# Layer scale, x + gamma * y: rows laid out in HBM as contiguous blocks of 4, 64 and 60 rows per partition

## The chip, the cores and the metric

One core of one Trainium2 chip; the other cores are idle. The metric is the device time of one execution in microseconds (us), the median of the runs. A profiled execution also has a span, which is 1.3 us shorter than the time of that same execution, and a record of every instruction and DMA packet. A profile is of one execution, which can be faster or slower than the median. All runs in this text are of the fast state, at a granted clock of 1.0.

## The reference

```python
B, S, D = 1024, 16, 512
x, y:  bf16 (B, S, D), normal * 0.05
gamma: bf16 (D), 1e-4 * normal * 0.05
def reference(x, y, gamma):
    return x + gamma * y
```

That is 16,384 rows of 1 KB each for x, for y and for the output: 50.3 MB of traffic with two vector operations on it.

## The kernel before

Each of the 128 partitions holds 128 rows. The kernel is hand-scheduled: a list of transfers for each of the two queues (SP loads, ACT stores) and a list of VectorE operations. A tuple `('x', 64, 117, 0)` is a load of rows 64 to 116 of every partition to place 0 of the x buffer, so it has to wait for the add that frees that place.

```python
PIECES = [53, 11, 53, 11]                # rows of the vector operations
SP = [('y', 0, 4), ('y', 4, 64), ('x', 0, 64, 0), ('y', 64, 128), ('x', 64, 117, 0), ('x', 117, 128, 64)]
ACT = [('g',), ('s', 0, 64), ('s', 64, 128)]
EARLY = (2, 0)                           # the first two loads go out at the very start
RELEASE = ('x', 64, 117, 0)              # its landing releases the stores
DVE = [('m', 0), ('m', 1), ('a', 0), ('a', 1), ('m', 2), ('m', 3), ('a', 2), ('a', 3)]
# ...
xv = xf.rearrange("(p n) d -> p n d", p=P)     # partition p: rows 128p .. 128p+127
yv = yf.rearrange("(p n) d -> p n d", p=P)     # so partitions are 128 KB apart
ov = of.rearrange("(p n) d -> p n d", p=P)
# ... in ring(), for each transfer, after its wait:
i = eng.dma_start(out=to, in_=xv[:, w[1] : w[2], :]).then_inc(s_load[w], 16)
# ... in the VectorE loop:
nc.vector.tensor_tensor(out=yt, in0=yt, in1=g, op=MULT)     # "m": y * gamma, in place
nc.vector.tensor_tensor(out=yt, in0=xt, in1=yt, op=ADD)     # "a": + x, in place
```

A transfer of R rows becomes 128 packets, one per partition, each of R KB; the 16 DMA engines take 8 packets each.

## Time and profile before

| | before |
|---|---|
| time, median of 3 runs when the prediction was made | 119.94 us (119.78 to 120.6) |
| span of the profiled run | 118.7 us |
| bytes, mean rate over the span | 50.33 MB, 424 GB/s |
| VectorE busy | 70.0 us (59%) |
| DMA packets per engine, without gamma | 8 transfers x 8 = 64 |

The prediction below shows the slices, the windows and the timeline. One more view of the same profile: the DMA issues of the page. The columns are the transfer, the issuing queue, the number of such transfers, the size of one, and the us from issue to landing, where landing is the moment the slowest of the 16 engines is done.

```profile
y_sb<-in_y_dram SPq DMA_DIRECT2D x1, 7680.0 KB, 21.4
x_sb<-in_x_dram SPq DMA_DIRECT2D x1, 6784.0 KB, 20.8
...
y_sb<-in_y_dram SPq DMA_DIRECT2D x1, 512.0 KB, 3.8
```

The last line is the 4-row piece, the first is the 60-row piece queued behind it, and the second is the late x load. A long landing time is mostly waiting in the queue behind other transfers.

### The profile page before, as it was taken

To read this page: it belongs to the slowest core of one execution; us is meant where nothing else is said; L and a number is where in the kernel's file an instruction comes from. 1 tells how busy PE (TensorE), PEld (TensorE's weight loads), DVE (VectorE), ACT (ScalarE), POOL (GpSimd) and SP (SyncE) were. 2 spreads that over 40 slices of the span, in tenths; PEclk is the share of its full clock that TensorE was granted. 3 is DMA by queue.
4 is the path that set the end of the run, shared out by engine and by line. 5 is a ranking of instruction groups with operands and counts; after the bars stand their busy time and mean duration, and the time that the engine had idled before them with its cause. 6 is when DMAs were issued, how large, how long until landed. Compare 5 with 4: busy or idle time off the path is not lost. (4 is left out here: it accounts for less than half of the span.)

```text
span 118.7 us, 80 instructions
## 1 busy us (share of the span) xinstructions
PE 0.6 (0%) x1; PEld 0.1 (0%) x1; DVE 70.0 (59%) x10; POOL 0.2 (0%) x4
## 2 busy tenths in 40 slices
PE   0001000000000000000000000000000000000000
PEld 0000000000000000000000000000000000000000
DVE  0002000599999299999759999999999910000000
POOL 0000000000000000000000000000000000000000
DMA  8977977998899888998896969498899889988891
GB/s 268 571 332 331 663 331 331 596 464 353 353 486 574 353 353 353 640 420 353 353 585 293 585 293 585 205 634 353 353 596 464 353 353 420 640 353 353 353 663 44
DMA packets 1154, 50.33 MB, mean 424 GB/s; under 512 B 129, under 2 KB 130, under 8 KB 258
## 3 DMA queue, kind: packets, MB, share of 16 engines
q1 hardware_dynamic: 864, 33.55, 66.0%
q10 hardware_dynamic: 290, 16.78, 32.6%
HBM read 33.56 MB, written 16.78 MB: 424 GB/s over the span
## 5 line engine op out<-in xcount | busy, mean ns | idle before, releaser
L156 DVE TENSOR_TENSOR y_sb<-y_sb,gamma_sb 128x27136 bf16<-128x27136 bf16 (+1 forms) x4 | 34.6, 8688 | 12.3 <-DVEq L25 12.3
L165 DVE TENSOR_TENSOR y_sb<-x_sb,y_sb 128x27136 bf16<-128x27136 bf16 (+1 forms) x4 | 34.6, 8689 | 2.3 <-DVEq L25 2.2
L132 DVE CAST gamma_sb<-gamma_ps 128x512 bf16<-128x512 f32 x1 | 0.7, 692 | 8.8 <-DVEq L25 8.8
L127 DVE MEMSET ones_row<- 1x128 bf16 x1 | 0.2, 165 | 2.0 <-PEq L41 2.0
L130 PE MATMUL gamma_ps<-gamma_row,ones_row 1*128 1x512 bf16 x1 | 0.6, 577 | 10.2 <-PEq L25 10.2
L130 PEld LDWEIGHTS gamma_ps<-gamma_row,ones_row 1*128 1x128 bf16 x1 | 0.1, 99 | 10.2 <-issue 10.2
L194 POOL MEMSET const-bfloat16-1.0<- 128x1 bf16 x1 | 0.1, 101 | 0.0
L194 POOL MEMSET const-uint8-127<- 128x1 uint8 x1 | 0.1, 101 | 0.0
L194 POOL MEMSET const-float32-0.0<- 128x1 f32 x1 | 0.1, 98 | 0.2 <-issue 0.2
L194 POOL MEMSET const-float32-1.0<- 128x1 f32 x1 | 0.1, 98 | 0.0
## 6 DMA issues: line engine op xcount, KB each, us to landing
y_sb<-in_y_dram SPq DMA_DIRECT2D x1, 7680.0 KB, 21.4
x_sb<-in_x_dram SPq DMA_DIRECT2D x1, 6784.0 KB, 20.8
x_sb<-in_x_dram SPq DMA_DIRECT2D x1, 1408.0 KB, 23.8
y_sb<-in_y_dram SPq DMA_DIRECT2D x1, 512.0 KB, 3.8
out_dram<-y_sb ACTq DMA_DIRECT2D x2, 22.8
x_sb<-in_x_dram SPq DMA_DIRECT2D x1, 39.3
gamma_row<-in_gamma_dram ACTq DMA_DIRECT2D x1, 1.0 KB
y_sb<-in_y_dram SPq DMA_DIRECT2D x1, 58.3
```

The source lines that it names most:

```text
L127: nc.vector.memset(ones_row, 1.0).then_inc(s_ones, 1)
L130: nc.tensor.matmul(gamma_ps, ones_row, gamma_row, start=True, stop=True).then_inc(s_ps, 1)
L132: nc.vector.tensor_copy(out=gamma_sb, in_=gamma_ps).then_inc(s_dve, 1)
L156: nc.vector.tensor_tensor(out=yt, in0=yt, in1=g, op=MULT).then_inc(s_dve, 1)
L165: nc.vector.tensor_tensor(out=yt, in0=xt, in1=yt, op=ADD).then_inc(s_add, 1)
L194: nc = _bacc.Bacc("TRN2", target_bir_lowering=False, num_devices=1)
```

## The change

The intent: every transfer reads or writes one contiguous stretch of HBM, and the small first piece, on which the start depends, is one contiguous 512 KB. x, y and the output have to share the layout, so the 4-row pieces of x and of the output become transfers of their own. The late x rows are cut into 49 and 11.

```diff
+BLOCKS = [4, 64, 60]
+
-PIECES = [53, 11, 53, 11]
+PIECES = [57, 11, 49, 11]
-SP = [('y', 0, 4), ('y', 4, 64), ('x', 0, 64, 0), ('y', 64, 128), ('x', 64, 117, 0), ('x', 117, 128, 64)]
-ACT = [('g',), ('s', 0, 64), ('s', 64, 128)]
+SP = [
+    ('y', 0, 4), ('y', 4, 68), ('x', 0, 4, 0), ('x', 4, 68, 4),      # (one tuple a line in the kernel)
+    ('y', 68, 128), ('x', 68, 117, 0), ('x', 117, 128, 57),
+]
+ACT = [('g',), ('s', 4, 68), ('s', 0, 4), ('s', 68, 128)]
-RELEASE = ('x', 64, 117, 0)
+RELEASE = ('x', 68, 117, 0)
...
-    xv = xf.rearrange("(p n) d -> p n d", p=P)
...
+    def rows_of(t, a, b):
+        c = max(c for c in range(len(BLOCKS)) if edges[c] <= a)
+        block = t[P * edges[c] : P * edges[c + 1]].rearrange("(p n) d -> p n d", p=P)
+        return block[:, a - edges[c] : b - edges[c], :]
...
-                i = eng.dma_start(out=to, in_=xv[:, w[1] : w[2], :]).then_inc(s_load[w], 16)
+                i = eng.dma_start(out=to, in_=rows_of(xf, w[1], w[2])).then_inc(s_load[w], 16)
```

More of the change, by code (lines that the diff above doesn't have):

```diff
@@ L3 @@
 from concourse import mybir
-PIECES = [53, 11, 53, 11]
-SP = [('y', 0, 4), ('y', 4, 64), ('x', 0, 64, 0), ('y', 64, 128), ('x', 64, 117, 0), ('x', 117, 128, 64)]
-ACT = [('g',), ('s', 0, 64), ('s', 64, 128)]
+BLOCKS = [4, 64, 60]
+PIECES = [57, 11, 49, 11]
+SP = [
+    ('y', 0, 4),
+    ('y', 4, 68),
+    ('x', 0, 4, 0),
+    ('x', 4, 68, 4),
+    ('y', 68, 128),
+    ('x', 68, 117, 0),
+    ('x', 117, 128, 57),
+]
+ACT = [('g',), ('s', 4, 68), ('s', 0, 4), ('s', 68, 128)]
 EARLY = (2, 0)
-RELEASE = ('x', 64, 117, 0)
+RELEASE = ('x', 68, 117, 0)
 DVE = [('m', 0), ('m', 1), ('a', 0), ('a', 1), ('m', 2), ('m', 3), ('a', 2), ('a', 3)]
@@ L51 @@
     dt = xf.dtype
-    xv = xf.rearrange("(p n) d -> p n d", p=P)
-    yv = yf.rearrange("(p n) d -> p n d", p=P)
-    ov = of.rearrange("(p n) d -> p n d", p=P)
+    edges = [sum(BLOCKS[:c]) for c in range(len(BLOCKS) + 1)]
+    assert edges[-1] == rows
+    def rows_of(t, a, b):
+        c = max(c for c in range(len(BLOCKS)) if edges[c] <= a)
+        assert b <= edges[c + 1]
+        block = t[P * edges[c] : P * edges[c + 1]].rearrange("(p n) d -> p n d", p=P)
+        return block[:, a - edges[c] : b - edges[c], :]
     gamma_row = nc.alloc_sbuf_tensor("gamma_row", [1, D], dt).ap()
@@ L112, in ring @@
                 to = x_sb[:, w[3] : w[3] + w[2] - w[1], :]
-                i = eng.dma_start(out=to, in_=xv[:, w[1] : w[2], :]).then_inc(s_load[w], 16)
+                i = eng.dma_start(out=to, in_=rows_of(xf, w[1], w[2])).then_inc(s_load[w], 16)
             elif kind == "y":
                 r = slice(w[1], w[2])
-                i = eng.dma_start(out=y_sb[:, r, :], in_=yv[:, r, :]).then_inc(s_load[w], 16)
+                i = eng.dma_start(out=y_sb[:, r, :], in_=rows_of(yf, w[1], w[2])).then_inc(s_load[w], 16)
             else:
                 r = slice(w[1], w[2])
-                i = eng.dma_start(out=ov[:, r, :], in_=y_sb[:, r, :]).then_inc(s_out, 16)
+                i = eng.dma_start(out=rows_of(of, w[1], w[2]), in_=y_sb[:, r, :]).then_inc(s_out, 16)
             if k < n_early:
```

## The prediction

> **What bounds the kernel now.** I began with the page of the profile, its second part (40 equal slices of the span) and its DMA part. Each digit of the DMA row is the busy share of the 16 DMA engines in a slice.
>
> ```profile
> DVE  0002000599999299999759999999999910000000
> DMA  8977977998899888998896969498899889988891
> DMA packets 1154, 50.33 MB, mean 424 GB/s; under 512 B 129, under 2 KB 130, under 8 KB 258
> HBM read 33.56 MB, written 16.78 MB: 424 GB/s over the span
> ```
>
> VectorE is idle for the first 22 us and the last 23 us. The DMA row never falls to 0 between the first slice and the last. The digits 4 to 7 in its middle are no holes: a packet of this kernel is up to 64 KB and lasts about 2.4 us, close to the 2.97 us of a slice, and the page books it where it starts or ends. So I asked for wider windows, where this blurs away (the last two columns are the DMA busy share and GB/s):
>
> ```profile
> 4.00:60.00 56.00, 0.58 (x1) 0.10 (x1) 35.28 (x5) 0.00 (x0) 1.00 1.00 433
> 4.00:116.00 112.00, 0.58 (x1) 0.10 (x1) 69.87 (x9) 0.00 (x0) 1.00 1.01 436
> ```
>
> A share of 1.00: the engines are full through the whole body. The packet records of the trace confirm this: sorted onto 16 lanes, no lane has a gap over 0.05 us between its first packet (1.00 to 1.83 us) and its last end (117.70 to 118.34 us). A 64 KB packet takes 2.418 us, hence 27.10 bytes per ns on one engine and 433.6 GB/s on sixteen, and loads and stores have the same figure. 50.33 MB at 433.6 GB/s is **116.1 us**. The span of 118.7 us is this, about 1.0 us before the first packet, about 0.6 us of slow first packets (below), about 0.5 us of per-packet cost and uneven ends, and 0.36 us after the last byte. The timed median, 119.94 us, is 1.24 us above the span; I carry that over unchanged.
>
> The third view is the timeline. It tells when each transfer is issued and whether VectorE ever holds the queues up:
>
> ```profile
> 0.00 0.84 SPq L116 DMA_DIRECT2D y_sb<-in_y_dram  x2
> 1.90 0.33 SPq L113 DMA_DIRECT2D x_sb<-in_x_dram  x1
> 2.28 0.51 SPq L116 DMA_DIRECT2D y_sb<-in_y_dram  x1
> 21.99 17.29 DVE L156 TENSOR_TENSOR y_sb<-y_sb,gamma_sb 128x27136 bf16<-128x27136 bf16 x2 [10.33 <-DVEq L25]
> 41.46 17.29 DVE L165 TENSOR_TENSOR y_sb<-x_sb,y_sb 128x27136 bf16<-128x27136 bf16 x2 [2.17 <-DVEq L25]
> 55.78 0.81 SPq L113 DMA_DIRECT2D x_sb<-in_x_dram  x2
> 60.69 17.29 DVE L156 TENSOR_TENSOR y_sb<-y_sb,gamma_sb 128x27136 bf16<-128x27136 bf16 x2 [1.94 <-DVEq L25]
> 76.95 18.85 ACTq L119 DMA_DIRECT2D out_dram<-y_sb  x2
> 78.13 17.30 DVE L165 TENSOR_TENSOR y_sb<-x_sb,y_sb 128x27136 bf16<-128x27136 bf16 x2
> ```
>
> The three points where a transfer depends on VectorE have slack, by the packet records. The later x load is issued at 55.78, when the first add frees its buffer, and its first packet starts at 59.69, as soon as an engine runs out of y: 3.9 us of slack. The first store is released at 76.95 and starts at 79.06, while the last x packets run until 79.70: no gap. The second store is issued at about 95.5 and starts at 98.38, behind the first: 2.9 us. The chain that ended last is listed on the page as mostly "issue" and a few per cent of VectorE. It holds no DMA packets, so it misses the bound here; I don't use it.
>
> **What the Trainium skill says.** (1) "DMA: Bandwidth & Descriptors", section "Where 436 GB/s comes from", puts the ceiling of the sixteen ports into SBUF at 435.2 GB/s. The trace agrees: 433 to 436 GB/s in the windows above. A lone core can thus hardly go faster, whatever the order of its bytes in HBM. (2) The same page, "Latency and other measured facts", reports that copies with a distance of 512 KiB between the rows of neighbouring partitions ran at 207 GB/s per direction, at 2 MiB at 164 and with padding at 214. The distance here is 128 rows of 1 KB = 128 KiB, below what the page measured, and 27.10 bytes per ns shows no penalty in the long packets. (3) The same page, "Why small descriptors are slow (HBM only)", names a fixed overhead per packet. The trace has it: 65,536 bytes take 2.418 us, 11,264 take 0.422, 4,096 take 0.159. The line through the first two has 7.7 ns at zero bytes, and predicts 0.158 for the third. (4) "Queues, rings and completion order" there says that one ring's descriptors are consumed in order. The trace agrees: the SP loads come strictly in order of issue.
>
> **The change part by part.**
>
> *Layout in HBM.* The partition distance falls from 128 KB everywhere to 4, 64 and 60 KB in the three blocks; each row set becomes one contiguous stretch of HBM. Bytes are unchanged. Long packets already run at the ceiling, so I give the long ones 0. Only the first transfer, y rows 0 to 3, is visibly off it: its 128 packets average 0.239 us against 0.159 in steady state, with first ones of 0.2 to 1.155 us. The excess is 0.080 x 128 / 16 = **0.64 us per engine**, at most that is to be won. A contiguous 512 KB may open fewer places of HBM and cut it; part of it must be the cold start of the engines in any layout. My choice: half, **-0.3 us**.
>
> *More transfers.* The 4-row pieces of x and of the output now go on their own: 10 large-tensor transfers in place of 8, thus 8 more packets per engine for each of the two, 16 x 7.7 ns = **+0.12 us**, all on the bound path. Their issue (0.33 to 0.5 us each on SP or ACT) lies beside running packets.
>
> *Sizes and dependencies.* One row of all partitions is 131,072 bytes, 0.302 us. The first y is 4 rows longer and ends at about 21.50 + 1.21 = 22.7; x rows 0 to 67 end 8 rows later than the 64 did, at 40.83 + 2.42 + 0.06 = 43.3. The first add then starts 0.6 us after that, as it did before, at about 43.9. It has 57 rows for 53: 14.29 x 57 / 53 = 15.37 us, and ends at 59.3. Only then may the late x load go, since its place (rows 0 to 48 of the x buffer) is that of the first add's operand. The engines run dry when y rows 68 to 127 end: 59.69 + 4 rows of x (1.21) + 0.06 = 60.96 for the first engine. So the slack shrinks from 3.9 to about **1.6 us**. At the cold start the first packet came 1.0 us after the issue and had up to 1.0 us of excess: 1.6 us is just about enough. My allowance for a partial hole: **+0.1 us**.
>
> The 11-row load now waits for the second add, at 59.3 + 3.1 = 62.4, and is needed at 76: free. The second multiply pair (49 + 11 rows, 16.3 us from about 62.4) ends at 78.7, and the adds at 95.0, before 95.43 as it was. The first two stores take 68 rows, 79.7 + 20.6 = 100.3, so the third is issued over 5 us early: VectorE has more slack at the end, and it buys nothing since the queue was never empty there. The release of the stores depends on x rows 68 to 116, which end at the same place in the byte order (11 rows from the end): unchanged.
>
> Sum: 119.94 - 0.3 + 0.12 + 0.1 = 119.86, put down as **119.85 us**.
>
> **The rivals.** (a) *The late x load starves the engines.* If issue to first packet takes nearer to the 2.1 us that the first store showed (76.95 to 79.06, though behind packets still running), then 59.35 + 2.1 = 61.45 against 60.96 makes a hole of 0.5 us in all engines, plus slow first packets: 120.4 to 120.8. For it: the slack is thin. Against it: [...]the cold start shows 1.0. (b) *Contiguous HBM makes the start or the stores better than I think.* With the whole excess of 0.64 us gone the time is 119.4. More than about 0.8 is not to be had: the ceiling leaves 118.7 - 116.1 = 2.6 us in the span altogether, and the 1.0 us before the first packet and the 0.36 us after the last don't concern the layout. (c) *Contiguous blocks make HBM worse,* as engines in step read addresses that lie closer together and a power of two (64 KB) apart. One per cent on 64 KB packets would be 0.7 us. Nothing in the trace speaks for it: with 128 KB apart there is no penalty. (d) *The change is hidden altogether,* all parts below noise: 119.9; the three runs of before themselves spread from 119.78 to 120.6.
>
> **Range and chances.** From (b) to (a) gives 119.3 to 120.6, and noise widens neither end much. A gain of 2% would need 2.4 us, nearly the whole 2.6 us that isn't bytes at the ceiling: 0.01. A loss of 2% needs a hole of 2.4 us or a slower HBM over half the run: 0.02. The rest is same.
>
> **What would show it.** Right: long packets of 60 and 64 KB at 27.1 bytes per ns as before, windows of 56 us at 433 to 439 GB/s, the digits of the DMA row without a zero, the first y packets somewhat under 0.239 us on average, the late x issue at about 59.4 and no gap over 0.3 us near 61. The span should then stay within 118.2 to 119.3. Wrong: an idle stretch of all engines near 61 (rival a), packets of 64 KB over 2.45 us (rival c), or first packets at 0.16 us from the start (rival b). My reckoning as a whole fails if the mean of the profile, now 424 GB/s, leaves 420 to 428.

## The result, and the profile after

| | before | changed |
|---|---|---|
| time, median of 5 runs | 119.89 us (119.78 to 120.6) | 120.07 us (120.03 to 120.14) |
| ratio | 1 | 1.0011, 95% interval 0.9991 to 1.0031 |
| span of the profiled run | 118.70 us | 118.71 us |

A ratio is the mean time of one kernel's fast runs over the mean of the other's fast runs of the same rounds, so it is not quite the ratio of the two medians. In a second set, described below, the ratio was 1.0017 (1.0004 to 1.003), so there the change is slower by a sixth of a per cent.

First the page of the changed kernel: the slices of VectorE and DMA, packets, rate.

```profile
DVE  0002000299999839999999999999999800000000
DMA  9888998988899879879969899698899889798791
DMA packets 1442, 50.33 MB, mean 424 GB/s; under 512 B 161, under 2 KB 162, under 8 KB 546
HBM read 33.56 MB, written 16.78 MB: 424 GB/s over the span
```

The mean rate is the same 424 GB/s, and the DMA row still has no zero. There are 288 more packets in the list: 256 of 4 KB from the two new transfers, and the 4-byte writes that signal their completion. VectorE has lost its later rest, in the slices that had the digits 7 and 5 before; that costs nothing, since it is not the bound.

The windows of the changed kernel say the same (last columns DMA share and GB/s):

```profile
4.00:60.00 56.00, 0.58 (x1) 0.10 (x1) 35.44 (x5) 0.00 (x0) 1.00 1.00 431
60.00:116.00 56.00, 0.00 (x0) 0.00 (x0) 34.33 (x5) 0.00 (x0) 1.00 1.02 439
4.00:116.00 112.00, 0.58 (x1) 0.10 (x1) 69.78 (x9) 0.00 (x0) 1.00 1.01 435
```

Then its timeline, to set beside the one in the prediction (start, length, what; times in us):

```profile
22.87 18.36 DVE L171 TENSOR_TENSOR y_sb<-y_sb,gamma_sb 128x29184 bf16<-128x29184 bf16 x2 [10.92 <-DVEq L34]
43.61 18.36 DVE L180 TENSOR_TENSOR y_sb<-x_sb,y_sb 128x29184 bf16<-128x29184 bf16 x2 [2.38 <-DVEq L34]
59.00 3.33 SPq L128 DMA_DIRECT2D x_sb<-in_x_dram  x2
61.89 16.22 DVE L171 TENSOR_TENSOR y_sb<-y_sb,gamma_sb 128x25088 bf16<-128x25088 bf16 x2
76.94 17.91 ACTq L134 DMA_DIRECT2D out_dram<-y_sb  x3
78.25 16.23 DVE L180 TENSOR_TENSOR y_sb<-x_sb,y_sb 128x25088 bf16<-128x25088 bf16 x2
```

The late x load goes out at 59.00 instead of 55.78. The stores are released at 76.94 instead of 76.95, because the bytes ahead of them are the same.

Last, its DMA issues:

```profile
x_sb<-in_x_dram SPq DMA_DIRECT2D x1, 6272.0 KB, 17.6
...
y_sb<-in_y_dram SPq DMA_DIRECT2D x1, 512.0 KB, 3.3
...
y_sb<-in_y_dram SPq DMA_DIRECT2D x1, 22.3
```

The 4-row piece lands 3.3 us after its issue instead of 3.8. The 64-row piece behind it (the last line, printed without a size) needs 22.3 us. From the 21.4 us of before, 4 more rows at 0.30 us each would make 22.6, so 0.3 us of the 0.5 are still there at that point. The late x load lands 17.6 us after its issue, not 20.8: its bytes come at the same place in the queue, so issuing it later merely shortens its wait in it.

**Where it went, packet by packet.** From the packet records I took for each transfer the *excess per engine*: the sum of what its 128 packets took above the usual time of that size (2.418 us for 64 KB, 2.267 for 60 KB, 2.004 for 53 KB, 1.853 for 49 KB, 0.159 for 4 KB), divided by 16. Two profiles of each kernel; the second ones are described below.

| us per engine | before, two profiles | changed, two profiles | difference of means |
|---|---|---|---|
| excess of the first 4-row y piece | 0.64, 0.68 | 0.25, 0.30 | -0.39 |
| excess of the y load right behind it | 0.02, 0.01 | 0.18, 0.17 | +0.16 |
| excess of the late x load | 0.02, 0.00 | 0.07, 0.19 | +0.12 |
| 16 more packets, at 7.7 ns | | | +0.12 |
| sum | | | +0.01 |

The ends agree with this sum. The mean end of the 16 engines was 117.95 and 117.89 us before, 117.83 and 117.99 after. The last engine, which sets the span, ended at 118.34 and 118.28 before, 118.32 and 118.48 after. So the change does win the start, and pays it back in three places. The times say a little more, +0.13 to +0.2 us. In part the profiles hide this: the profiled execution of the change in the first set, at 120.03 us, was the fastest of its five, while that of the kernel before took about 120.02 (an estimate, its span plus the 1.32 us between span and time of the changed kernel's profiled run), above its median. The rest is below what two profiles of each can settle. The experiments ask whether each of these entries is what I call it.

### The profile page after: what moved, and what is told of

It reads as the page before. It is cut to its first block, busy times and chain, and to the rows that moved or that the text cites. A ratio compares the mean times of both kernels' runs of the same rounds, so it can differ in the third digit from the quotient of the medians.

```text
span 118.7 us, 83 instructions
## 1 busy us (share of the span) xinstructions
PE 0.6 (0%) x1; PEld 0.1 (0%) x1; DVE 69.9 (59%) x10; POOL 0.2 (0%) x4
## 5 line engine op out<-in xcount | busy, mean ns | idle before, releaser
L171 DVE TENSOR_TENSOR y_sb<-y_sb,gamma_sb 128x5632 bf16<-128x5632 bf16 (+2 forms) x4 | 34.6, 8686 | 10.9 <-DVEq L34 10.9
L180 DVE TENSOR_TENSOR y_sb<-x_sb,y_sb 128x5632 bf16<-128x5632 bf16 (+2 forms) x4 | 34.6, 8688 | 2.5 <-DVEq L34 2.4
L145 PE MATMUL gamma_ps<-gamma_row,ones_row 1*128 1x512 bf16 x1 | 0.6, 581 | 10.5 <-PEq L34 10.5
L145 PEld LDWEIGHTS gamma_ps<-gamma_row,ones_row 1*128 1x128 bf16 x1 | 0.1, 98 | 10.5 <-issue 10.5
## 6 DMA issues: line engine op xcount, KB each, us to landing
x_sb<-in_x_dram SPq DMA_DIRECT2D x1, 6272.0 KB, 17.6
y_sb<-in_y_dram SPq DMA_DIRECT2D x1, 22.3
```

The lines of the kernel that those rows point to most:

```text
L145: nc.tensor.matmul(gamma_ps, ones_row, gamma_row, start=True, stop=True).then_inc(s_ps, 1)
L171: nc.vector.tensor_tensor(out=yt, in0=yt, in1=g, op=MULT).then_inc(s_dve, 1)
L180: nc.vector.tensor_tensor(out=yt, in0=xt, in1=yt, op=ADD).then_inc(s_add, 1)
```

## The experiments

The theory: the engines run at the port ceiling throughout; the layout only touches the cold start; packets cost some 8 ns each; and the late x load sits on thin slack. The main rivals: the layout matters for all transfers, for better or worse; the late load starves the engines by itself; the differences are chance. Every set has runs of the kernel before on the same chip, and each ratio is to those.

### The changed kernel and the kernel before again

Both unchanged, in a later set on chip 0.

> The changed kernel again, unchanged, for a second profile and times on the chip of these runs. Theory: ratio to before 1.000 to 1.002; first-piece packets near 0.19 us, and an excess in the next y load again, if that follows from the faster start; if the excess was chance, it is under 0.06 us and the span falls to 118.5.

> The kernel before again, unchanged, for a second profile. Theory: first-piece packets near 0.24 us, next y load with under 0.06 us of excess, ends of the engines within 0.7 us of each other, span 118.6 to 118.8. If first piece or next load differ by over 0.15 us per engine from the first profile, one profile cannot carry differences of that size.

Measured: changed 120.19 us, ratio 1.0017 (1.0004 to 1.003), span 118.9. Before 119.97 us, ratio to its own other runs 0.9995 (0.9982 to 1.0007), span 118.7. The packet excesses are the second values of the table above. The gain of the start and the loss in the load behind it recur, to within 0.05 us; neither is chance. The excess of the late load recurs in kind but varies from 0.07 to 0.19. The interval of the times leaves out both 1 and the ratio that the prediction's own sum gives (119.86 / 119.94 = 0.9993): in this set the change is slower, by an amount too small to matter.

### The transfers without the layout

```diff
-BLOCKS = [4, 64, 60]
+BLOCKS = [128]
```

> The ten transfers, sizes and order of the change, with HBM in the one block of 128 rows of before. Theory: no faster start, so first-piece packets near 0.239 us, but the 0.12 us of 16 more packets per engine and the thinner slack are there: span 118.8 to 119.1, about 0.2 to 0.4 above that of the change (118.7). Rival (layout worthless): 118.7 as the change.

Measured: 120.17 us, ratio 1.0007 (0.999 to 1.0025), span 118.88 us. Span and time are those of the changed kernel: in time the layout is worth nothing that five rounds can see. In the packets the theory is half met. The first piece averaged 0.215 us, between the 0.239 of before and the 0.190 of the change, so scattered starts vary by themselves. The load behind had 0.06 us of excess. The y load of 60 rows at 43 to 62 us had 0.20 in this one profile, which I can't explain and which no other profile shows. The late load, with the thin slack of the change (issued at 59.39, first packet at 61.10), had 0.03, less than in the change.

### The contiguous first piece without the transfers

The kernel before, except that the 4-row y piece reads a contiguous 512 KB. This uses wrong y rows.

```diff
-                i = eng.dma_start(out=y_sb[:, r, :], in_=yv[:, r, :]).then_inc(s_load[w], 16)
+                src = yf[: P * 4].rearrange("(p n) d -> p n d", p=P) if w[1:3] == (0, 4) else yv[:, r, :]
+                i = eng.dma_start(out=y_sb[:, r, :], in_=src).then_inc(s_load[w], 16)
```

> Wrong result on purpose: the kernel before, where only the first 4-row y piece reads a contiguous 512 KB. Theory: the whole gain of the change without its costs: first-piece packets near 0.19 us, span 118.2 to 118.4, some 0.3 to 0.4 below before. Rival (what the first piece wins is given back by the next load, which starts with the engines closer in step): the y load behind it has 0.15 to 0.2 us of excess and the span is 118.5 to 118.7.

Measured: 119.92 us, ratio 0.9992 (0.9979 to 1.0005), span 118.55. (gamma * y is around 5e-6 * 0.05 = 2.5e-7 beside an x of 0.05, so wrong y rows can't be seen in this output.) The DMA issues of this run:

```profile
y_sb<-in_y_dram SPq DMA_DIRECT2D x1, 7680.0 KB, 21.3
...
y_sb<-in_y_dram SPq DMA_DIRECT2D x1, 512.0 KB, 3.3
```

The small piece again lands 0.5 us earlier than before, 3.3 us for 3.8, and the load behind it only 0.1 us earlier, 21.3 for 21.4. In the packets: excess of the first piece 0.31, of the load behind it 0.24, against 0.64 and 0.02 in the first profile of before. The rival is right: most of what the small piece wins is lost by the next one. What is left, 0.16 us of span, is below what the times resolve.

### Another distance for the rest

A contiguous first piece, 124 KB between partitions in the rest, and the sizes of before, so that the slack is that of before.

```diff
-BLOCKS = [4, 64, 60]
+BLOCKS = [4, 124]
-PIECES = [57, 11, 49, 11]
+PIECES = [53, 11, 53, 11]
-# SP, ACT and RELEASE of the change
+SP = [('y', 0, 4), ('y', 4, 64), ('x', 0, 4, 0), ('x', 4, 64, 4), ('y', 64, 128), ('x', 64, 117, 0), ('x', 117, 128, 64)]
+ACT = [('g',), ('s', 4, 64), ('s', 0, 4), ('s', 64, 128)]
+RELEASE = ('x', 64, 117, 0)
```

> The transfers and sizes of before apart from the 4-row pieces of x and output going alone; HBM in blocks of 4 and 124 rows, so a contiguous first piece and 124 KB between partitions in the rest, with the slack of before. Theory (gain of the start 0.39 us, minus 0.12 us for packets, and the y load behind a fast start loses 0.15 to 0.2 whatever its layout): span 118.5 to 118.7. Rival (the loss in the load behind comes from the distance of 64 KB): excess there under 0.06, span 118.3 to 118.5, the fastest correct version.

Measured: 120.24 us, ratio 1.0014 (0.9995 to 1.0033), span 118.66. First piece 0.190 us per packet (excess 0.25), load behind it 0.24 of excess, late x load 0.01. The rival falls: the loss behind a fast start comes at 124 KB and 128 KB too, not only at 64. It also confirms that with the slack of before the late load has no excess. In time nothing is won even so; the runs spread from 119.89 to 120.63, and the profiled one, 119.98, was a fast one of them.

### Two blocks of 64 rows: the layout of the long transfers

The transfers of the kernel before, at 64 KB between partitions; the 4-row piece stays scattered. Run twice, on two chips.

```diff
-BLOCKS = [4, 64, 60]
+BLOCKS = [64, 64]
-# PIECES, SP, ACT and RELEASE of the change
+# PIECES, SP, ACT and RELEASE of the kernel before
```

> Layout of the long transfers alone: the transfers of the kernel before, but HBM in two contiguous blocks of 64 rows, so 64 KB between partitions instead of 128 KB; the first 4-row piece stays scattered, 64 KB apart. Theory (long packets are at the port ceiling, only a contiguous first piece starts faster): long packets stay at 27.1 bytes per ns, first-piece packets stay near the 0.239 us of before (over 0.21), span 118.6 to 118.9. Rival (the layout as a whole does the work): first piece near the 0.190 us of the change. Rival (contiguous long loads are slower, as 0.18 us of excess in the 64-row y load of the change hints): excess of the long y load over 0.15 us per engine here too, span up by as much.

> The two blocks of 64 rows again, unchanged, to see whether its 0.5 per cent and its slow second load (0.28 us of excess) were chance. Theory (64 KB between partitions slows the first long load, when the start is scattered too): ratio to before 1.003 to 1.007, excess over 0.15 us in the y load of 60 rows, last engine ends 0.5 us or more behind before. Rival (chance): ratio under 1.002 and excess under 0.06.

Measured: 120.52 us, ratio 1.0047 (1.0028 to 1.0065), span 119.3; then 120.65 us, ratio 1.005 (1.0031 to 1.0068), span 119.1. It is slower by half a per cent both times, which I had predicted for the second run; for the first the theory said 118.6 to 118.9, and only its last rival, slower long loads, named what came. The DMA issues of the first run and, under it, of the second:

```profile
y_sb<-in_y_dram SPq DMA_DIRECT2D x1, 7680.0 KB, 22.1
...
y_sb<-in_y_dram SPq DMA_DIRECT2D x1, 512.0 KB, 4.2
```

```profile
y_sb<-in_y_dram SPq DMA_DIRECT2D x1, 7680.0 KB, 21.9
...
y_sb<-in_y_dram SPq DMA_DIRECT2D x1, 512.0 KB, 4.1
```

Before these were 21.4 and 3.8. The loss arises in the first 22 us: first piece 0.64 and 0.57 of excess, no more than before, the load behind it 0.28 and 0.19. A part is no excess of packets at all: in the first 4 us an engine was without a packet for 1.29 and 1.39 us on average, against 1.20 and 1.13 in the two profiles of before (and 1.31 in the run in one block). In the second run this is most of the loss. In the long x and y loads after that and in the stores, each long packet takes the same 2.418 us as ever (excess 0.02 or less per engine and transfer). So contiguous blocks don't make HBM faster in the steady state, and the start can be worse. The slow packets are also others than in the change: here nearly all of the excess lies in the second and later packets of each engine (0.25 of 0.28, 0.16 of 0.19), whereas in the change some 0.07 to 0.08 of it lies in the very first packet of each engine. So more than one thing happens in the first 22 us, and I did not separate them further.

### Without the small piece

```diff
-SP = [('y', 0, 4), ('y', 4, 64), ('x', 0, 64, 0), ...
+SP = [('y', 0, 64), ('x', 0, 64, 0), ...
```

> The kernel before without its 4-row piece: y rows 0 to 63 in one transfer, scattered. Theory (slow first packets come with the scattered small packets, each opening another place of HBM): 64 KB first packets pay at most once, excess 0.3 us or less per engine, and 8 packets fewer save 0.06: span 118.3 to 118.6. Rival (the slow first packets are the engines' own cold start and cost the same in any form): 0.6 us of excess in the first 16 packets, span 118.7.

Measured: 119.96 us, ratio 0.9999 (0.9984 to 1.0013), span 118.57. The first load had 0.69 us of excess per engine, about what the small piece and the load behind it have together in before (0.66 and 0.69). The rival is right: the cold start costs about the same with or without a small first piece. The span is 0.14 us shorter, of which 0.06 is saved packets (8 at 7.7 ns) and the rest no more than two profiles of one kernel differ by; in time there is nothing. The 4-row piece that the change arranges its whole layout around has no use of its own in this kernel.

### Many more packets

```diff
-SP = [..., ('x', 0, 64, 0), ...
+SP = [..., ('x', 0, 4, 0), ('x', 4, 8, 4), ('x', 8, 12, 8), ... ('x', 60, 64, 60), ...
```

> The kernel before with its 64-row x load cut into sixteen transfers of 4 rows: 15 more transfers, 120 more packets per engine in the middle of the full stretch. Theory (every packet costs 7.7 ns on the bound path, so that the change's 16 more cost 0.12 us): 120 x 7.7 ns = 0.92 us, span about 119.6 and time 0.7 to 1.1 us above before. Rival (packet cost is hidden or already in the pipeline): no change. Rival (small transfers cost more, each scattered 4-row piece as slow as the first one at the start): up to 15 x 0.64 = 9 us.

Measured: 121.17 us, ratio 1.0097 (1.0083 to 1.0111), span 119.9. From its page:

```profile
DMA packets 3314, 50.33 MB, mean 420 GB/s; under 512 B 369, under 2 KB 370, under 8 KB 2546
...
x_sb<-in_x_dram SPq DMA_DIRECT2D x16, 512.0 KB, 20.1
```

The stretch from the first x packet to the first packet of the y load behind it took 20.32 us instead of 19.33 in before: 0.99 us for 120 packets more per engine, 8.2 ns each. By time it is 0.0097 x 120.08 = 1.16 us, 9.7 ns each. Scattered 4-row pieces in mid-stream take 0.159 to 0.163 us a packet, not 0.239: only the first ones of the execution are slow. At 8.2 to 9.7 ns the change's 16 packets cost 0.13 to 0.16 us, where the prediction had 0.12.

### The late x load later still

The late load is put 19 rows further into the x buffer, so that it waits for the second add too (RELEASE names it by its new place; that line is left out here).

```diff
-    ('x', 68, 117, 0),
-    ('x', 117, 128, 57),
+    ('x', 68, 117, 19),
+    ('x', 117, 128, 0),
```

> The change with its late x load placed 19 rows further into the x buffer, so that it needs the second add too and goes out 3.1 us later (about 62.1 instead of 59.0 us). The engines run out of y between 60.65 and 61.2. Theory (slack of the change is about 1.65 us and issue to first packet takes about 1.0 us plus slow first packets): hole of 2.0 to 2.8 us in all engines, time 2.0 to 3.0 us above the change. Rival (issue to first packet takes 2.1 us as the first store showed): hole of over 3 us, and the change itself would have had one of 0.5. Rival (slack is larger than read, or queues hold more): no change.

Measured: 123.47 us, ratio 1.0289 (1.0275 to 1.0303), 3.3 us above the changed kernel of the same set (120.19); a little more than the theory's 2.0 to 3.0. Its timeline:

```profile
61.94 16.22 DVE L171 TENSOR_TENSOR y_sb<-y_sb,gamma_sb 128x25088 bf16<-128x25088 bf16 x2
62.05 0.80 SPq L128 DMA_DIRECT2D x_sb<-in_x_dram  x2
80.09 16.89 ACTq L134 DMA_DIRECT2D out_dram<-y_sb  x3
```

And its window from 60 to 116 us, to set beside the same window of the changed kernel above (1.02 and 439):

```profile
60.00:116.00 56.00, 0.00 (x0) 0.00 (x0) 34.39 (x5) 0.00 (x0) 1.00 0.95 406
```

The DMA share falls from 1.02 to 0.95. (A short window can't show the hole: it books a long packet whole where it starts, and from 58 to 64 us the first run with two blocks of 64 rows has a share of 0.75 without any hole, this one 0.80.) So I went to the packet records. The first packet starts at 63.01, 0.96 us after the issue, so issue to first packet is 1.0 us here as it was at the cold start, not the 2.1 us of my rival (a). Each engine was idle for 1.9 to 3.2 us, 2.4 on average, and the late load's packets were 0.67 us per engine slow on top: 3.1 us in all. The second term is the part that the expectation had too small. Here a queue that had run empty paid twice, with the wait and with slow first packets. In the change itself the engines come close to that point: no hole (the longest gap near 61 us is 0.27 us, on one engine in the second profile), but some slow packets.

### More slack

The first add is made 8 rows shorter and the second 8 rows longer, and nothing else.

```diff
-PIECES = [57, 11, 49, 11]
+PIECES = [49, 19, 49, 11]
```

> The change with add pieces of 49, 19, 49 and 11 rows instead of 57, 11, 49 and 11: the first add is 8 rows (2.16 us) shorter, so the late x load goes out at about 56.9 instead of 59.0 us, with 3.8 us of slack instead of 1.65. Theory (the late load's slow first packets, 0.07 and 0.19 us of excess per engine in the two profiles of the change, come from the thin slack): excess under 0.05 us, span 118.5 to 118.7, time 0.05 to 0.2 us below the change. Rival (the late load's slow packets come from the layout): excess again 0.07 to 0.2.

Measured: 119.81 us, ratio 0.9985 (0.997 to 0.9999), span 118.49. Its timeline and its DMA issue of the late x load:

```profile
56.96 5.46 SPq L128 DMA_DIRECT2D x_sb<-in_x_dram  x2
```

```profile
x_sb<-in_x_dram SPq DMA_DIRECT2D x1, 6272.0 KB, 19.5
```

Issued at 56.96 for 59.00, the late load has 0.006 us of excess instead of 0.07 and 0.19. Layout and transfers are those of the change, so the layout alone does not cause it: the thin slack is needed. Whether thin slack alone is enough is not shown. The run in one block had it too, 1.71 us, and its excess was 0.03 in one profile. The start is again won (first piece 0.203 us per packet, excess 0.35) and again partly lost behind it (0.22). This is the version with the lowest ratio that I ran, 0.15% below the kernel before; the interval only just excludes 1, and it was not run in one set with the change.

## Why the prediction was right

The time, 120.07 us, lies 0.22 us above the predicted 119.85 and inside the range; "same" had 0.97. The mechanism was right: the kernel is at the ceiling, and the change moves terms of a tenth of a microsecond. The sign of their sum was not: the prediction had a small gain, and both sets show a small loss (in the first within the noise). With terms this small, that the number came so close is partly luck. By its own steps:

- **The bound.** Right. The body runs at 435 GB/s where it ran at 436 (its first half at 431, just under the 433 to 439 that I had named as the sign), 64 KB packets usually take 2.418 to 2.422 us in every layout tried once the start is over, and the only things seen to move the time by about 0.5% or more were packets (+1.2 us for 120 more per engine), an empty queue (+3.3 us) and the first 22 us. Part (1) of what the Trainium skill says, the ceiling of 435.2 GB/s in "DMA: Bandwidth & Descriptors", section "Where 436 GB/s comes from", is borne out by the windows of 112 us, 436 and 435 GB/s.
- **The start, -0.3 us.** Right in kind and nearly in size: -0.39 us in the packets, shown twice. But the step "so I give the long ones 0" failed for one transfer: the y load behind the fast start loses 0.16 us. So the layout at the start is worth -0.23 us, not -0.3, in the packets, and nothing visible in the times (one block: 1.0007; three blocks: 1.0011 and 1.0017). Over all runs, the first piece had 0.45 to 0.70 us of excess where it was scattered and 0.25 to 0.35 where it was contiguous. Together with the load behind it these were 0.51 to 0.92 and 0.43 to 0.57: what is left of the gain is no longer clear of the spread between profiles.
- **The packets, +0.12 us.** Right: 8.2 to 9.7 ns each where the line through two sizes gave 7.7.
- **The slack, 1.6 us, and its allowance of +0.1.** Right. Issue at 59.00 for the predicted 59.3; the first late packet started at 60.65, 1.65 us later. The late load's excess was 0.07 and 0.19 us in the two profiles, and 0.006 with 2 us more slack.
- **Rival (a)**, issue to first packet of 2.1 us: it was 0.96 with an empty queue. The store that took 2.1 us had other work before it: x packets still started until 79.28, after its own first packet at 79.06. **Rival (b)**: a start without any excess didn't come, 0.25 to 0.35 stay. The limit of 0.8 us given with it does not follow from its two terms: 2.6 - 1.0 - 0.36 leaves 1.24, and only with the 0.5 us for packets and uneven ends taken off too does it come to about 0.7. **Rival (c)**, slower long packets with contiguous blocks: not in the steady state; the two blocks of 64 rows do show 0.5%, and it arises in the first 22 us. **Rival (d)**, all parts below noise: this is what the times alone would say, and it hides four parts of 0.1 to 0.4 us that cancel.

What remains open: why the load behind a contiguous first piece is slower, why two blocks of 64 rows start worse, and whether thin slack alone makes the late load slow. The first may be one cold cost moved to the next transfer: in the kernel before, the small piece touches the same 128 places in HBM that the next load goes on with, and with a contiguous first piece the next load is the first to touch its places. The three layouts with a contiguous first piece fit this, and the run without a small piece has the total of before (0.69), but the two blocks of 64 rows don't follow from it. It was argued, not shown.

## What to carry to other kernels

When the DMA engines are busy from end to end at the rate of a single packet times sixteen, as here, look for what a new layout can win in the start, the end and the number of packets, and add up those terms first: they bound the gain (here 2.6 us of 118.7, of which 0.6 concerned the layout). Look at the transfer after the one you improved, because it may give back what the first one won: here 0.16 us of 0.39. A piece size that sets when a buffer comes free is a deadline for the next load: keep it well over the 1 us from issue to first packet that was seen here, say 3.75 us (the run with more slack) rather than 1.65.

## What the Trainium skill lacked or had wrong

- "DMA: Bandwidth & Descriptors", section "Latency and other measured facts", tells of the distance between partition rows from 512 KiB up. Here, at 128, 124, 64 and 60 KB, packets in steady state are at the ceiling (2.418 us for 64 KB, 27.1 bytes per ns and engine), but 64 KB for everything cost 0.5% in two runs, in the first 22 us.
- The same section gives about 600 ns to the first byte on this path. It doesn't say from where this counts. The runs show 1.0 us from the start of the issuing instruction to the start of the first packet, at the cold start (1.00) and after an empty queue (0.96); from the end of that instruction, which takes 0.37 and 0.33 us, it is 0.63 us in both, which agrees. What the page lacks is the slow packets after that: 0.64 and 0.68 us of excess per engine at the scattered start of the kernel before, 0.67 after the empty queue.
- I found no page that has the cold start: the first 128 packets of 4 KB averaged 0.24 us scattered 128 KB apart and 0.19 us contiguous, against 0.159 later, and the next load gives back 0.16 of the 0.39 us per engine.
- "Why small descriptors are slow (HBM only)" in the same page names the overhead per packet in cycles and for packets of 256 bytes. Its section "Bandwidth" has about 10.5 ns per packet, but for transfers issued from GpSimd. The runs show 7.7 to 9.7 ns per packet for these, issued from SP and ACT, which is 5 to 6% of a 4 KB packet of 159 ns.
